# One block of full-row products, r turned in the outputs' banks, scores in quarters, and a growing lookahead in a recurrence followed by experts

## The chip, the cores and the metric

The kernel runs on one core of a Trainium2 chip. The metric is the device time of one execution in microseconds. A core has a matrix engine (PE, with its weight loads counted apart as PEld), a vector engine (DVE), a scalar engine (ACT), a general engine (POOL) and a queue engine (SP) that issues transfers. Each engine works through its own instructions in the order in which the program gives them, and semaphores make one engine wait for another.

## What is computed

Two blocks follow each other. The first is a recurrence over 768 tokens for 4 batches and 8 heads of 48 elements, with a state that decays by `w` and a bonus `u` for the token's own term:

```python
for t in range(S):
    kt, vt, rt = (k[:, :, t], v[:, :, t], r[:, :, t])
    cur = np.einsum('bhd,bhe->bhde', u[None] * kt, vt)
    y[:, :, t] = np.einsum('bhd,bhde->bhe', rt, state + cur)
    state = w[None, :, :, None] * state + np.einsum('bhd,bhe->bhde', kt, vt)
```

Its output, seen as 3072 rows of 384, goes to a mixture of 16 experts in 4 groups of 4. Each row picks the best group and in it the best expert, and gets `combined * relu(x @ w1) @ w2` of that expert alone, where `combined` is the product of the two softmax weights.

```python
g_idx = np.argmax(g_logits, axis=1)
...
e_idx = np.argmax(e_logits, axis=1)
...
h = np.maximum(xg[mask_e] @ w1[g, e], 0.0)
ye = h @ w2[g, e]
...
out[tok_idx] = combined[:, None] * ye
```

## The kernel before, in words

The order of instructions on each engine is the order in which the program writes them; no scheduler moves them. Waits on PSUM go by what was written or read there before.

*The recurrence.* The tokens are cut into 24 blocks of 128, four batches by six stretches of time. Block `n` belongs to batch `n % 4`, and two neighbouring blocks form a pair whose `r`, `k` and `v` are loaded together. One step `s` of the main loop (L708) finishes block `s` and prepares later ones. For each block these pieces are needed:

- `scaled` (POOL): k divided by the decay, into `kp`. `own` (POOL): r times k times u, in two products, into `dg`.
- `turn(n, "kT")` and `turn(n, "rT")` (L442): four 128x128 transposes on PE each, into the bank `TR`; `turn_out` copies k out with ACT and multiplies r by the decay `pw` with DVE.
- `sum_own` (L435, DVE): sums `dg` over a head's elements to `du`, the token's own term. `diagonal(n, e)` (L480, ACT): four products each that write identity times `du` into `am`, so that a block has eight.
- `scores` (L460, PE): eight products of k by r, 48 rows deep, two of them side by side in the upper and lower half of the rows, into `PA`. `mask` (L470, DVE): copies the later tokens' scores over `am`, which has the diagonal by then.
- `state` (L489, PE): the carried state times r, into `YB`. `values` (L501, PE): `am` times v, added to it. `update` (L510, PE): k times v, into the bank `MS`. `carry` (L521, DVE): decays and adds the state. `values_out` (L532, ACT): copies `YB` to `yT`.

*The routing.* `rows_out` (L547) transposes `yT` back into rows (`RW`) and ACT copies them to `xt`. `gate_parts` (L536) multiplies `yT` by the gates' weights into the first 128 columns of `MS`, ACT copies that to `lT`, and `gate_sum` (L563) adds its four parts into the logits, other columns of `MS`. Every four steps a chunk of 512 rows is routed by `route_1` to `route_4` on DVE, with `route_e` on ACT and `route_p` on PE. `route_5` scatters the rows into regions of `x_sorted` by POOL, one tile per step from a list `late`. `fill` writes zeros into the ends of the regions, on SP, in steps 1 to 4.

*The experts.* From step 16 the first two experts' weights are requested piece by piece. After the last routing the 16 experts run one after the other, `up` (L868) and `down` (L883), with rows gathered by SP and results scattered by POOL.

PSUM has eight banks: `PA` and `YB` two each, `TR`, `RW`, `MS` and `SB` one each. In `YB` the results take 256 of 512 columns of each bank (`y_ps`).

In the loop before, a steady step gives PE: results, update, turn k of block `s + 3`, rows of block `s - 1`, scores of block `s + 2`, gate parts, turn r of block `s + 3`, prefix sums if due, gate sum of block `s`, state of block `s + 1`. DVE gets: carry, the own term's sum for `s + 3`, routing, mask, turned r. ACT gets: copy of the results, turned k, rows, four diagonal products, `lT`, four diagonal products. Step 0 also prepares block 2, and in steps 0 and 1 the sum comes after the turn of r (`begun`, L756).

Of the kernel before, what the change touches and what calls it, by code (L numbers as in the profile page):

```python
# [13 lines left out]
OP = mybir.AluOpType  # L14
# [3 lines left out]
P = 128  # L18
# [9 lines left out]
def kernel(  # L28
# [13 lines left out]
    nc = tc.nc  # L42
# [180 lines left out]
    with ExitStack() as rec:  # L223
# [11 lines left out]
        MS = ps([P, 512], "MS")  # L235
        SB = ps([P, 512], "SB")
        y_ps = YB[:, :, 0 : 2 * P]

        spare_at = [0]

# [37 lines left out]
        def load_half(t, src, g, a, queue):  # L278
            c, b = g // 2, 2 * (g % 2) + a
            queue.dma_start(out=t[:, a], in_=src[b, :, P * c : P * (c + 1), :].rearrange("h t d -> t h d"))  # L280
# [16 lines left out]
        for a in range(2):  # L297
            load_half(raw[0, "k"], k, 0, a, both[a])
            load_half(raw[0, "r"], r, 0, a, both[1 - a])
        zeros = ring.tile([P, XW], FP32, name="zeros")  # L300
        warm = ring.tile([P, 1], FP32, name="warm")
        nothing = ring.tile([P, 1], FP32, name="nothing")
        nc.vector.memset(nothing, 0.0)
        nc.scalar.activation(warm, nothing, AF.Exp)
        nc.scalar.dma_start(
            out=ub.rearrange("p h d -> p (h d)"), in_=bass.AP(tensor=u.tensor, offset=u.offset, ap=[[0, P], [1, H * D]])
        )
        raw[0, "v"] = load(v, 0, "vt", 4)
        raw[1, "r"] = load(r, 1, "rt", 3)
        raw[1, "k"] = load(k, 1, "kt", 3)  # L310
# [63 lines left out]
        def fill(i):  # L374
            for lo in range(FILL[0], FILL[1], 64):
                nc.sync.dma_start(
                    out=xs_reg[4 * i : 4 * i + 4, lo : lo + 64, :].rearrange("e n w -> n e w"),
                    in_=spread(zeros[64 * (i % 2) : 64 * (i % 2 + 1)], 1, 4),
                )
# [60 lines left out]
        turned = {}  # L440

        def turn(n, name, bank=None, early=False):  # L442
            ps = turned[n, name] = TR if bank is None else bank
            src = (kp if name == "kT" else rp)[(n // 2) % NKP]
            for hc in range(HC):
                two = src[:, n % 2, 2 * hc : 2 * hc + 2, :].rearrange("p e x -> p (e x)")
                nc.tensor.transpose(ps[:, hc, :], two, ident)  # L447
            if not early:
                turn_out(n, name)

        def turn_out(n, name):
            ps = turned.pop((n, name))
            dst = pool.tile([P, HC, P], FP32, tag=name, bufs=5 if name == "rT" else 4, name=name)
            rkT[n, name] = dst
            if name == "kT":
                nc.scalar.copy(dst, ps)  # L456
            else:
                nc.vector.tensor_tensor(out=dst, in0=ps, in1=pw, op=OP.mult)  # L458

        def scores(n):  # L460
            kT, rT = rkT.pop((n, "kT")), rkT[n, "rT"]
            for hc in range(HC):
                for e in range(2):
                    rows = slice(DP * e, DP * e + D)
                    nc.tensor.matmul(  # L465
                        PA[:, e, P * hc : P * (hc + 1)], lhsT=kT[rows, hc, :], rhs=rT[rows, hc, :],
                        start=True, stop=True, skip_group_check=True,
                    )

        def mask(n):  # L470
            nc.vector.copy_predicated(  # L471
# [4 lines left out]
        def diagonal_here(n):  # L476
            du = dus[n].rearrange("p (hc e) -> p e hc", e=2)
            nc.vector.copy_predicated(am[n % NAM][:, 0], spread(id_ps, 1, HC).bitcast(I32), spread(du[:, 0], 2, P))

        def diagonal(n, e):  # L480
            du = dus[n].rearrange("p (hc e) -> p e hc", e=2)
            for hc in range(HC):
                nc.scalar.mul(am[n % NAM][:, e, hc, :], ident, du[:, e, hc : hc + 1])  # L483
# [48 lines left out]
        def values_out(n):  # L532
            yT = yTs[n] = pool.tile([P, 2, 2, P], FP32, tag="yT", bufs=3, name="yT")
            nc.scalar.copy(yT.rearrange("p e j t -> p e (j t)"), y_ps)  # L534

        def gate_parts(n):  # L536
            yT = yTs[n]
            for q in range(NQ):
                e, j = q // 2, q % 2
                nc.tensor.matmul(  # L540
                    MS[32 * q : 32 * (q + 1), 0:P], lhsT=gwp[:, 4 * j + e, :], rhs=yT[:, e, j, :],
                    start=True, stop=True, skip_group_check=True,
                )
            lT = mid[n] = pool.tile([P, P], FP32, tag="lT", bufs=3, name="lT")
            nc.scalar.copy(lT, MS[:, 0:P])

        def rows_out(n):  # L547
            yT = yTs[n]
# [136 lines left out]
        turn_out(0, "rT")  # L685
        scaled_here(0, 1)
        nc.scalar.copy(T2, RWT)
        turn(1, "rT", YB[:, 0].rearrange("p (h t) -> p h t", t=P))
        sum_own(0)
        diagonal_here(0)  # L690
        scores(0)
        turn(1, "kT")
        diagonal(0, 1)
        mask(0)
        own(0, 1)
        scaled(1, 0)
# [5 lines left out]
        own(1, 1)  # L702
        scaled(2)
        same = ring.tile([P, HC], FP32, name="same")
        LA = 3
        late = []
        left = []
        for s in range(NT):  # L708
            g = s // 2 + 2
            if s % 2 == 0 and g < NG:  # L710
                if g + 1 < NG:
                    raw[g + 1, "k"] = load(k, g + 1, "kt", 3)
                    raw[g + 1, "r"] = load(r, g + 1, "rt", 3)
                raw[g, "v"] = load(v, g, "vt", 4)
            for job in left[0 : 1 if s < 18 else 2]:
                job()
            del left[0 : 1 if s < 18 else 2]
            if s % 2 == 0 and g < NG:
                if g > 2:
                    scaled(g)  # L720
                own(g, None, 0)
            if s % 2 == 1 and g < NG:
                own(g, None, 1)
            for c, i in late[0 : 1 if s < 22 else 2]:
                route_5(c, (i,))
            del late[0 : 1 if s < 22 else 2]
            if s == 0:
                nc.gpsimd.memset(zeros, 0.0)
            if s == 1:
                late_consts()  # L730
            if s == 3:
                consts()
            if s == 5:
                last_consts()
            if s in (1, 2, 3, 4):
                fill(s - 1)
            far = s + LA < NT
            values(s)
            update(s)
            values_out(s)  # L740
            for c in range(NB - 1):
                if s == 4 * c + 5:
                    route_e(c)
            carry(s)
            if s == 0:
                sum_own(1)
                diagonal_here(1)
                diagonal(1, 1)
                scores(1)
                mask(1)  # L750
                turn(2, "kT")
                turn(2, "rT")
                sum_own(2)
                diagonal(2, 0)
                diagonal(2, 1)
            begun = s >= 2  # L756
            if far:
                turn(s + LA, "kT")
                if begun:
                    sum_own(s + LA)  # L760
            if s >= 1:
                rows_out(s - 1)
            for c in range(NB - 1):
                last = c == NB - 2
                if s == 4 * c + 4:
                    route_1(c)
                if s == 4 * c + 5:
                    route_2(c)
                if s == 4 * c + 6:
                    route_3(c)  # L770
                    if c == 2:
                        choose_two()
                if s == 4 * c + (6 if last else 7):
                    route_4(c)
                    late += [(c, i) for i in range(4)]
            if s == 15:
                for i in range(2):
                    e = at_sp(two_i[0:1, i : i + 1])
                    early[i] = weight_tiles()
                    left += [partial(early_piece, e, *early[i], j) for j in range(NPIECE)]  # L780
            if s + 2 < NT:
                scores(s + 2)
                mask(s + 2)
            if far and begun:
                diagonal(s + LA, 0)
            gate_parts(s)
            if far:
                turn(s + LA, "rT")
                if not begun:
                    sum_own(s + LA)  # L790
                    diagonal(s + LA, 0)
                diagonal(s + LA, 1)
            for c in range(NB - 1):
                if s == 4 * c + 5:
                    route_p(c)
                    if c == 2:
                        count(12)
            gate_sum(s)
            if s + 1 < NT:
                state(s + 1)  # L800
            if s == 0:
                nc.vector.tensor_tensor(out=same, in0=wcol, in1=wraw, op=OP.not_equal)
        c = NB - 1
        rows_out(NT - 1)
        for job in late:
            route_5(job[0], (job[1],))
# [397 lines left out]
```

## Time and profile before

| | |
|---|---|
| median of 3 runs | 445.26 us (443.38 to 446.50) |
| profiled execution | 445.16 us, span 443.4 us |
| granted PE clock | 0.966 of full speed on average |
| first results of the recurrence | 17.7 us |
| results of step 4, of step 20 | 48.7 us, 138.2 us |
| results of the last step | 151.8 us |
| first product of the experts | 171.8 us |
| last scatter of an output begins | 439.0 us |

Work of the four compute engines by stage (busy us, from the windows of the profile):

| stretch, us | PE | DVE | ACT | POOL | PE clock |
|---|---|---|---|---|---|
| 0 to 17.7 | 6.76 | 10.66 | 6.03 | 12.47 | half |
| 17.7 to 30 | 10.68 | 5.06 | 5.54 | 8.36 | half |
| 30 to 48.7 | 15.99 | 12.59 | 14.13 | 16.43 | full from 30.7 |
| 48.7 to 138.2 | 87.02 | 63.60 | 66.40 | 49.40 | full |
| 138.2 to 152 | 12.81 | 7.55 | 7.00 | 5.18 | full |
| 152 to 172 | 5.31 | 8.72 | 5.07 | 7.32 | half from 157 |
| 172 to 443 | 258.36 | 42.74 | 88.40 | 103.94 | full from 177.5 |

A line of the timeline gives the start in us from the span's start, the duration, the engine, the line of the kernel, the operation, the tile written and the tiles read, and the number of instructions merged; in brackets stands how long the engine had been idle before and whose end released it. The page cuts the span into 40 slices of 11.1 us, one digit each, in tenths of busy time.

### The profile page before, as it was taken

The page shows a single profiled execution, that of the slowest core. Times are in us where ns is not written, and L with a number is a line of the kernel's source. Part 1 is how long each engine was busy: PE and PEld are TensorE (multiplying, and loading weights), DVE is VectorE, ACT ScalarE, POOL GpSimd, SP SyncE. Part 2 cuts the span into 40 slices and gives each one's busy share as a digit, 9 for nine tenths or more (in the row PEclk, how much of TensorE's full clock was granted, in tenths as well). Part 3 has the DMA queues.
Part 4 walks back from the last instruction along what each step waited for, and adds up shares of the span by engine and source line. Part 5 has one row for each costly group of instructions (what it writes and reads, how often), then busy time and mean ns, then how long its engine had stood idle before and what let it go on. Part 6 is the DMA issues. An engine that isn't in the chain of part 4 may idle for free.

```text
span 443.4 us, 9627 instructions
## 1 busy us (share of the span) xinstructions
PE 396.9 (90%) x3506; PEld 371.5 (84%) x3506; DVE 150.9 (34%) x389; ACT 192.6 (43%) x461; POOL 203.1 (46%) x240
## 2 busy tenths in 40 slices
PE   3787999999999825999999999999999999999980
PEld 2666787878788614999999999999999999999970
DVE  6456676767776362020220220220220122022110
ACT  3358777777777303234243244243244334423410
POOL 6689536666643331023614524524523633452435
PEclk9999999999999955999999999999999999999995
DMA  9899997731996627397798898899998999999000
GB/s 151 118 192 215 189 184 149 148 84 38 197 270 174 213 85 168 76 250 167 226 267 180 233 273 178 237 256 208 245 275 178 251 266 214 252 259 258 21 23 25
DMA packets 122902, 81.97 MB, mean 185 GB/s; under 512 B 96420, under 2 KB 114020, under 8 KB 122848
## 3 DMA queue, kind: packets, MB, share of 16 engines
q1 hardware_dynamic: 114976, 70.98, 70.6%
q0 software_dynamic: 4960, 9.55, 7.7%
q10 hardware_dynamic: 2912, 0.77, 1.0%
q8 instruction: 29, 0.48, 0.5%
q14 instruction: 25, 0.20, 0.2%
HBM read 70.09 MB, written 11.68 MB: 184 GB/s over the span
## 4 chain that ended last, share of the span: by engine, by line
issue 45%; PE 26%; POOL 16%; DVE 4%; DMA 4%; ACT 3%; POOLq 1%; DVEq 0%; ACTq 0%
POOL out_dram L900 16%; PE TR L447 6%; PE YB L505 5%; PE PA L465 5%; DMA out_dram<-yt,idn 3%; PE YB L496 3%; PE MS L540 2%; ACT am L483 2%; PE MS L516 2%; PE RW L550 1%; PE MS L564 1%; POOL x_sorted L215 1%; DVE du L438 1%; DMA x_sorted<-xt,place_i 1%; DMA wraw<-in_w_dram 0%
## 5 line engine op out<-in xcount | busy, mean ns | idle before, releaser
L900 POOL DMA_INDIRECT out_dram<-yt,idn x107 | 103.9, 971 | 167.4 <-DVE yt L898 125.4
L876 PE MATMUL ph<-xe,w 128*128 128x200 f32 (+12 forms) x768 | 133.2, 334 | 8.1 <-DMA w<-in_moe_w_dram 8.1
L876 PEld LDWEIGHTS ph<-xe,w 128*128 128x128 f32 x768 | 130.3, 193 | 8.7 <-issue 8.1
L888 PE MATMUL po<-hT,w2p 128*128 128x200 f32 (+12 forms) x768 | 130.4, 330 | 0.0
L888 PEld LDWEIGHTS po<-hT,w2p 128*128 128x128 f32 x768 | 128.1, 190 | 0.0
L897 DVE STREAM_TRANSPOSE yt<-yT 128x672 f32<-128x672 f32 (+1 forms) x16 | 13.6, 847 | 211.1 <-ACT yT L891 211.1
L881 ACT ACTIVATE hT<-ph 128x416 f32<-128x416 f32 (+12 forms) x64 | 31.9, 498 | 101.9 <-PE ph L876 100.4
L483 ACT ACTIVATE am<-ident,du 128x128 f32<-128x128 f32 x184 | 58.6, 397 | 7.6 <-DVE du L438 7.6
L866 ACT COPY w2p<-w 128x1024 f32<-128x1024 f32 x48 | 47.0, 1046 | 11.9 <-POOL yT L823 11.9
L215 POOL DMA_INDIRECT x_sorted<-xt,place_i x24 | 24.0, 998 | 50.4 <-issue 43.9
L891 ACT COPY yT<-po 128x208 f32<-128x208 f32 (+12 forms) x48 | 15.5, 323 | 69.2 <-PE po L888 67.3
L471 DVE COPY_PREDICATED am<-later,PA 128x1024 f32<-128x1024 int32 x24 | 31.3, 1304 | 13.3 <-PE PA L465 7.6
L465 PE MATMUL PA<-rT,kT 48*128 48x128 f32 x384 | 30.6, 304 | 0.0
L505 PE MATMUL YB<-am,vt 128*48 128x128 f32 x384 | 26.8, 283 | 3.2 <-DVE am L471 3.2
L465 PEld LDWEIGHTS PA<-rT,kT 48*128 48x128 f32 x384 | 25.7, 204 | 4.3 <-issue 3.7
L505 PEld LDWEIGHTS YB<-am,vt 128*48 128x48 f32 x384 | 20.5, 125 | 7.4 <-DVE am L471 3.6
L534 ACT COPY yT<-YB 128x512 f32<-128x512 f32 x24 | 14.0, 584 | 28.0 <-PE YB L505 28.0
L431 POOL TENSOR_TENSOR kp<-kt,T 128x768 f32<-128x768 f32 x10 | 18.3, 1830 | 9.1 <-PE MS L516 4.6
L456 ACT COPY kT<-TR 128x512 f32<-128x512 f32 x24 | 14.0, 583 | 12.5 <-PE TR L447 12.0
L421 POOL TENSOR_TENSOR dg<-rp,kt 128x768 f32<-128x768 f32 x10 | 18.3, 1826 | 1.0 <-DMA rp<-in_r_dram 1.0
L423 POOL TENSOR_TENSOR dg<-dg,ub 128x768 f32<-128x768 f32 x10 | 18.3, 1827 | 0.4
L447 PE MATMUL TR<-ident,kp 128*128 128x128 f32 x96 | 17.6, 311 | 0.9 <-DVE rT L458 0.9
(140 smaller groups left out, 317.9 us busy)
## 6 DMA issues: line engine op xcount, KB each, us to landing
w<-in_moe_w_dram SPq DMA_DIRECT2D x128, 384.0 KB, 8.5
vt<-in_v_dram SPq DMA_DIRECT2D x24, 192.0 KB, 5.2
kt<-in_k_dram SPq DMA_DIRECT2D x23, 192.0 KB, 4.6
rp<-in_r_dram SPq DMA_DIRECT2D x23, 192.0 KB, 5.2
xg<-x_sorted SPq DMA_DIRECT2D x42, 85.8 KB, 4.7
out_dram<-yt,idn POOLq DMA_INDIRECT x107, 4.9
x_sorted<-zeros SPq DMA_DIRECT2D x4, 392.0 KB, 5.0
xg<-x_sorted SPq DMA_DIRECT2D x20, 73.5 KB, 5.1
```

The lines of the kernel that those rows point to most:

```text
L215: ins = nc.gpsimd.indirect_dma_start(out=xs_dram, out_offset=bass.IndirectOffsetOnAxis(ap=place_i[:, i : i + 1], axis=0), in_=xt[:, i].rea ...
L421: nc.gpsimd.tensor_mul(dg, rt, kt)
L447: nc.tensor.transpose(ps[:, hc, :], two, ident)
L465: nc.tensor.matmul(PA[:, e, P * hc : P * (hc + 1)], lhsT=kT[rows, hc, :], rhs=rT[rows, hc, :], start=True, stop=True, skip_group_check=True,)
L471: nc.vector.copy_predicated(am[n % NAM], later.unsqueeze(1).unsqueeze(1).to_broadcast([P, 2, HC, P]).bitcast(I32), PA.rearrange("p e (h t) ...
L483: nc.scalar.mul(am[n % NAM][:, e, hc, :], ident, du[:, e, hc : hc + 1])
L505: nc.tensor.matmul(y_at(e, hc), lhsT=vt[:, n % 2, 2 * hc + e, :], rhs=amn[:, e, hc, :], start=(n < 4 and hc < 2), stop=True, skip_group_ch ...
L866: nc.scalar.copy(o4[:, kk], v4[:, kk])
L876: nc.tensor.matmul(ph[:, i, 0:n], lhsT=w1[:, ko, P * (f + i) : P * (f + i + 1)], rhs=xe[:, ko].rearrange("p i b -> p (i b)")[:, 0:n], star ...
L881: nc.scalar.activation(hTs[s][:, f : f + 2, 0:n], ph[:, :, 0:n], AF.Relu)
L888: nc.tensor.matmul(po[:, 0:n], lhsT=w2p[:, d, fo, :], rhs=hT[:, fo, 0:n], start=(fo == 0), stop=(fo == FO - 1))
L900: ins = nc.gpsimd.indirect_dma_start(out=out_q, out_offset=bass.IndirectOffsetOnAxis(ap=idn[:, i : i + 1].bitcast(U32), axis=0), in_=yt[:, ...
```

## The change

- `turn` puts r into columns 256 to 511 of the outputs' two banks (`RT` in `YB`) instead of `TR`.
- `gate_parts` writes into the first 128 columns of `TR` (`lT_ps`) instead of `MS`.
- `scores` makes four products of each former two: the left and the right 64 columns of k, the right ones against the right 64 columns of r alone. Block 0 stays as it was.
- The order of a step: after `carry` come turn k, rows, turn r, gate sum (of the block before), prefix sums and gate parts; then routing; then scores, mask and state; and last the own term (`own_term`: the sum, then eight diagonal products).
- Steps 0 to 2 turn block `s + 2`, and step 2 also block 5; scores are one block ahead in steps 1 and 2, and step 3 makes up for the one that lacks. From step 3 on the lookahead is as it was.
- The load of `u` is issued between two halves of the first loads on ACT's queue; in the preparation the diagonal of block 0 goes ahead of the turns of block 1.
- The fills move to steps 4 to 7, the prefix sums one step later, and the scatters are taken one per step and four in the last.

```diff
+        RT = YB[:, :, 2 * P : 4 * P].rearrange("p b (h t) -> p b h t", t=P)
+        lT_ps = TR[:, 0, :]
...
+            if a == 0:
+                nc.scalar.dma_start(
+                    out=ub.rearrange("p h d -> p (h d)"),
+                    in_=bass.AP(tensor=u.tensor, offset=u.offset, ap=[[0, P], [1, H * D]]),
+                )
...
-            ps = turned[n, name] = TR if bank is None else bank
+            ps = (TR if name == "kT" else RT) if bank is None else bank
...
+                    for z in range(2):
+                        nc.tensor.matmul(
+                            PA[64 * z : 64 * (z + 1), e, P * hc + 64 * z : P * (hc + 1)],
+                            lhsT=kT[rows, hc, 64 * z : 64 * (z + 1)], rhs=rT[rows, hc, 64 * z : P],
+                            start=True, stop=True, skip_group_check=True,
+                        )
...
-                    MS[32 * q : 32 * (q + 1), 0:P], lhsT=gwp[:, 4 * j + e, :], rhs=yT[:, e, j, :],
+                    lT_ps[32 * q : 32 * (q + 1), :], lhsT=gwp[:, 4 * j + e, :], rhs=yT[:, e, j, :],
...
-        turn(1, "rT", YB[:, 0].rearrange("p (h t) -> p h t", t=P))
         sum_own(0)
         diagonal_here(0)
+        diagonal(0, 1)
+        turn(1, "rT", YB[:, 0].rearrange("p (h t) -> p h t", t=P))
         scores(0)
         turn(1, "kT")
-        diagonal(0, 1)
         mask(0)
...
-            for c, i in late[0 : 1 if s < 22 else 2]:
+            for c, i in late[0 : 1 if s < NT - 1 else 4]:
                 route_5(c, (i,))
...
-            if s in (1, 2, 3, 4):
-                fill(s - 1)
+            if s in (4, 5, 6, 7):
+                fill(s - 4)
+
+            def own_term(n):
+                sum_own(n)
+                diagonal(n, 0)
+                diagonal(n, 1)
...
             if s == 0:
                 sum_own(1)
                 diagonal_here(1)
                 diagonal(1, 1)
+            values(s)
+            update(s)
+            values_out(s)
+            carry(s)
+            if s == 0:
                 scores(1)
                 mask(1)
...
+            if s == 3:
+                scores(4)
+                mask(4)
+            far = s + (3 if s > 2 else 2)
+            if far < NT:
+                turn(far, "kT")
             if s >= 1:
                 rows_out(s - 1)
...
+            if far < NT:
+                turn(far, "rT")
+            if s >= 1:
+                gate_sum(s - 1)
+            for c in range(NB - 1):
+                if s == 4 * c + 6:
+                    route_p(c)
+                    if c == 2:
+                        count(12)
+            gate_parts(s)
...
+            ahead = s + (2 if s > 2 else 1)
+            if 0 < s and ahead < NT:
+                scores(ahead)
+                mask(ahead)
             if s + 1 < NT:
                 state(s + 1)
+            if far < NT:
+                own_term(far)
+            if s == 2:
+                turn(5, "kT")
+                turn(5, "rT")
+                own_term(5)
...
+        gate_sum(NT - 1)
         rows_out(NT - 1)
```

More of the change, by code (lines that the diff above doesn't have):

```diff
@@ L304 @@
         nc.scalar.activation(warm, nothing, AF.Exp)
-        nc.scalar.dma_start(
-            out=ub.rearrange("p h d -> p (h d)"), in_=bass.AP(tensor=u.tensor, offset=u.offset, ap=[[0, P], [1, H * D]])
-        )
         raw[0, "v"] = load(v, 0, "vt", 4)
@@ L442, in turn @@
         def turn(n, name, bank=None, early=False):
-            ps = turned[n, name] = TR if bank is None else bank
+            ps = (TR if name == "kT" else RT) if bank is None else bank
+            turned[n, name] = ps
             src = (kp if name == "kT" else rp)[(n // 2) % NKP]
@@ L446, in turn @@
                 two = src[:, n % 2, 2 * hc : 2 * hc + 2, :].rearrange("p e x -> p (e x)")
-                nc.tensor.transpose(ps[:, hc, :], two, ident)
+                dst = ps[:, hc, :] if len(ps.shape) == 3 else ps[:, hc // 2, hc % 2, :]
+                nc.tensor.transpose(dst, two, ident)
             if not early:
@@ L456, in turn_out @@
                 nc.scalar.copy(dst, ps)
-            else:
-                nc.vector.tensor_tensor(out=dst, in0=ps, in1=pw, op=OP.mult)
+            elif len(ps.shape) == 3:
+                nc.vector.tensor_tensor(out=dst, in0=ps, in1=pw, op=OP.mult)
+            else:
+                nc.vector.tensor_tensor(
+                    out=dst.rearrange("p (b h) t -> p b h t", b=2), in0=ps,
+                    in1=pw.rearrange("p (b h) t -> p b h t", b=2), op=OP.mult,
+                )
         def scores(n):
@@ L464, in scores @@
                     rows = slice(DP * e, DP * e + D)
[L465 to L468, printed above, removed]
+                    if n == 0:
+                        nc.tensor.matmul(
+                            PA[:, e, P * hc : P * (hc + 1)], lhsT=kT[rows, hc, :], rhs=rT[rows, hc, :],
+                            start=True, stop=True, skip_group_check=True,
+                        )
+                        continue
+                    for z in range(2):
+                        nc.tensor.matmul(
+                            PA[64 * z : 64 * (z + 1), e, P * hc + 64 * z : P * (hc + 1)],
+                            lhsT=kT[rows, hc, 64 * z : 64 * (z + 1)], rhs=rT[rows, hc, 64 * z : P],
+                            start=True, stop=True, skip_group_check=True,
+                        )
         def mask(n):
@@ L544, in gate_parts @@
             lT = mid[n] = pool.tile([P, P], FP32, tag="lT", bufs=3, name="lT")
-            nc.scalar.copy(lT, MS[:, 0:P])
+            nc.scalar.copy(lT, lT_ps)
         def rows_out(n):
@@ L704 @@
         same = ring.tile([P, HC], FP32, name="same")
-        LA = 3
         late = []
@@ L723 @@
                 own(g, None, 1)
-            for c, i in late[0 : 1 if s < 22 else 2]:
+            for c, i in late[0 : 1 if s < NT - 1 else 4]:
                 route_5(c, (i,))
-            del late[0 : 1 if s < 22 else 2]
+            del late[0 : 1 if s < NT - 1 else 4]
             if s == 0:
@@ L734 @@
                 last_consts()
-            if s in (1, 2, 3, 4):
-                fill(s - 1)
[L737 to L744, printed above, removed]
+            if s in (4, 5, 6, 7):
[4 more added lines that the diff above has]
+                diagonal(n, 1)
             if s == 0:
@@ L748 @@
                 diagonal(1, 1)
+            values(s)
[3 more added lines that the diff above has]
+            if s == 0:
                 scores(1)
                 mask(1)
[L751 to L760, printed above, removed]
+            if s == 3:
[4 more added lines that the diff above has]
+                turn(far, "kT")
             if s >= 1:
@@ L763 @@
             for c in range(NB - 1):
-                last = c == NB - 2
+                if s == 4 * c + 5:
+                    route_e(c)
+            if far < NT:
[8 more added lines that the diff above has]
+            gate_parts(s)
+            for c in range(NB - 1):
                 if s == 4 * c + 4:
@@ L772 @@
                         choose_two()
-                if s == 4 * c + (6 if last else 7):
+                if s == 4 * c + (6 if c == NB - 2 else 7):
                     route_4(c)
@@ L780 @@
                     left += [partial(early_piece, e, *early[i], j) for j in range(NPIECE)]
[L781 to L798, printed above, removed]
+            ahead = s + (2 if s > 2 else 1)
+            if 0 < s and ahead < NT:
+                scores(ahead)
+                mask(ahead)
             if s + 1 < NT:
                 state(s + 1)
+            if far < NT:
[4 more added lines that the diff above has]
+                own_term(5)
             if s == 0:
```

## The prediction

> **What bounds the kernel now.** I read the page first (busy times, slices, chain), then the chain in order of time, then the timeline of one steady step and of step 1. From the page:
>
> ```profile
> span 443.4 us, 9627 instructions
> ...
> PE 396.9 (90%) x3506; PEld 371.5 (84%) x3506; DVE 150.9 (34%) x389; ACT 192.6 (43%) x461; POOL 203.1 (46%) x240
> ...
> PE   3787999999999825999999999999999999999980
> ...
> PEclk9999999999999955999999999999999999999995
> ```
>
> Two stages with a hollow between them. The slices are 11.1 us each. Slices 0 to 13 are the recurrence (its products run from 17.7 to 153 us), and from 171.8 us the experts keep PE busy to the end. The change touches the recurrence and the zero fills alone; the experts begin after the last scatter, so what the recurrence gains or loses moves the end one for one. The profiled execution took 445.16 us (443.4 span, 1.7 around it), 0.1 from the median of 445.26, so the sum needs no correction.
>
> PE and DVE in a steady step, from the timeline (start, duration):
>
> ```profile
> 89.24 0.66 PE L447 MATMUL TR<-ident,kp 128*128 128x128 f32 x4
> ...
> 89.73 0.60 PE L550 MATMUL RW<-ident,yT 128*128 128x128 f32 x4
> ...
> 90.09 0.54 DVE L438 TENSOR_REDUCE du<-dg 128x8 f32<-128x384 f32 x1
> ...
> 90.26 1.16 PE L465 MATMUL PA<-rT,kT 48*128 48x128 f32 x16
> ...
> 91.35 0.43 PE L540 MATMUL MS<-yT,gwp 128*32 128x128 f32 x8
> 91.54 1.32 DVE L471 COPY_PREDICATED am<-later,PA 128x1024 f32<-128x1024 int32 x1 [0.51 <-PE PA L465]
> ...
> 91.71 0.66 PE L447 MATMUL TR<-ident,rp 128*128 128x128 f32 x4
> ...
> 92.27 0.40 PE L564 MATMUL MS<-sel,lT 128*128 128x20 f32 x2
> ...
> 92.60 0.66 PE L496 MATMUL YB<-rT,R 48*48 48x128 f32 x16
> ...
> 93.18 1.08 PE L505 MATMUL YB<-am,vt 128*48 128x128 f32 x16
> ```
>
> PE never waits: its starts follow each other, and a step is 93.18 - 87.87 = 5.31 us. With the routing's steps the mean from step 4 to step 20 (48.7 to 138.2) is 5.60. The sum `du` runs on DVE before the mask (90.09 against 91.54), so ACT has it long before it fills the diagonal.
>
> Step 1, where today's code still sums late, shows what ACT does with a late `du`:
>
> ```profile
> 31.52 0.54 DVE L438 TENSOR_REDUCE du<-dg 128x8 f32<-128x384 f32 x1
> ...
> 32.10 2.45 ACT L483 ACTIVATE am<-ident,du 128x128 f32<-128x128 f32 x8 [2.01 <-DVE du L438]
> ...
> 34.45 0.56 ACT L534 COPY yT<-YB 128x512 f32<-128x512 f32 x1
> ...
> 34.92 0.58 ACT L456 COPY kT<-TR 128x512 f32<-128x512 f32 x1
> ...
> 35.06 0.16 PEld L540 LDWEIGHTS MS<-yT,gwp 128*32 128x32 f32 x8 [0.83 <-ACT yT L534]
> ```
>
> ACT idles 2.0 us for `du`, then does eight diagonal products, and only then copies out the results; PE waits for that copy.
>
> **The change, part by part.**
>
> *PE's order.* By starts, a step today is: results 0.91, state sums 0.46, turn k 0.49, rows 0.53, scores 1.09, gate parts 0.36, turn r 0.56, gate sum 0.33, carried state 0.58. In one block, rows, turn r and gate sum follow each other without a change of shape. A turn's four products are 0.11 apart (0.60 = 3 x 0.11 + 0.27), so rows and turn r are 0.44 each. The gate sum no longer waits for `lT`, which is a step old. The step's PE work is then 0.91 + 0.46 + 0.49 + 0.44 + 0.44 + 0.33 + 0.36 + scores + state.
>
> *Scores in quarters.* Eight products become sixteen. The nearest row is the carried state, four tiles at once, 16 instructions in 0.58, rounds of four 0.11 apart. Each row half still streams eight times 128 columns: 8 x 0.11 + 0.04 = 0.91. Bounds: 0.91, or half as much again (1.36) if the 64-column pieces do not run beside the others. I take 0.91, the carried state's form being nearly the same. State then follows in the same shape, 0.53. Sum 4.87 us, a gain of 0.44 if PE stays the limit.
>
> *The own term moves behind the mask.* This decides. Today `sum_own(s + 3)` stands ahead of routing and mask on DVE. After the change `own_term` comes last in the step: on DVE the sum is queued behind `mask(s + 2)`, the mask waits for `scores(s + 2)`, and these now come after `gate_parts(s)`, which needs `yT(s)`. On ACT the eight diagonal products wait for the sum, and behind them is queued `values_out(s + 1)`, which makes `yT(s + 1)`. Turn r, now in the outputs' banks, waits for that copy too (today the gate parts wait for DVE's reads elsewhere in their own bank, so the wait goes by banks). The ring closes once a step. Its length, each link from a row where the second waited for the first:
> yT to PE 0.61 (34.45 to 35.06); turn r to gate sum 0.49 (as turn k); gate sum 0.33; gate parts 0.36; scores to mask 1.2 (90.26 to 91.54, less 0.09 for the lighter first load); mask to the next on DVE 1.15 (86.28 to 87.43); sum to the first diagonal 0.58 (31.52 to 32.10); eight diagonals to yT 2.35 (32.10 to 34.45). Together 7.07 us a step, against 4.87 of PE work, which it hides.
>
> It runs in steps 3 to 20, 18 rounds: 127.3 us.
>
> *Routing.* In the ring DVE has 1.0 us between r's product and the mask. Route 1 takes 1.2 (+0.2, five times), route 2 1.67 (+0.66, four), route 3 and the choice of two +0.4. The prefix sums stand ahead of the gate parts on PE: 0.5 each, five times, and the count 0.3. Together 6.8. Today's reads of the logits that hold up the gate parts (2.1 us by the waits) go, but PE waits anyway.
>
> *The first steps.* `ub` is loaded about a microsecond sooner (POOL waits 2.0 us for it, ended at 9.49), and the diagonal of token block 0 is filled before k of block 1 is copied. The mask of step 0 then waits for the scores (13.5) in place of ACT (16.3), so its results begin near 14.9, not 17.7. Step 0 turns one pair fewer: step 1's results start at about 22.5 (30.9 today, where PE waits 1.3 us for POOL's scaled keys and turns two pairs). Steps 1 and 2 already run the ring, at half clock in part (about 8.5 each), and step 2 holds two own terms (16 products, 4.7 us): results of step 2 near 31.1, of step 3 near 39.6, scores of step 5 near 46.1. Today these begin at 45.8. The start's gain is eaten by then.
>
> *The end.* Steps 21 to 23 have no own term: from scores of step 23 to the results of step 23, 0.91 + 0.53, then copy, gate parts, state (1.8 + 0.36 + 0.55), 4.2 us. The four scatters go to step 23; POOL has 5.6 us idle there. The fills move from steps 1-4 to 4-7, on SP behind the loads, land in 5 us and are needed at step 8: nothing.
>
> *Sum.* Results of step 23 start at 46.1 + 127.3 + 6.8 + 4.2 = 184.4; today 151.8. So +32.6, and 445.2 + 32.6 = 478.
>
> *PE's clock* is not in it. In the ring PE waits 7.07 - 4.87 = 2.2 us in one piece each step. The trace has the clock fall at 157 us, after
>
> ```profile
> 154.69 0.64 PE L550 MATMUL RW<-ident,yT 128*128 128x128 f32 x4
> 156.77 0.52 PE L176 MATMUL MS<-ohe,later 128*128 128x64 f32 x2 [1.45 <-DVE ohe L167]
> ```
>
> when PE was busy 1.51 of 3.40 us; it kept full speed with 2.30 of 3.40 busy (41.0 to 44.4). The worst 3.4 us in the ring have about 1.2 to 1.5 busy, so it can fall in places. At half clock the ring's PE links grow by about 1.8 us (scores 2.0 for 1.1 at 27.09, turns 1.02 for 0.56). Bounds: 0 and 18 x 1.8 = 32; I take 0 for the likeliest, since a slowed PE fills its own wait and gets the clock back, as at 30.7, and keep up to 20 for the range.
>
> The Trainium skill (TensorE: Matmul & The Clock Gate, "Why this matters for your kernels") puts the fall at idle gaps of about 3 us. Here it fell after gaps of 1.5 us at most, so the row speaks for a fall that the rule would exclude; by the rule the sum stays 478.
>
> **The rivals.**
>
> *Faster: PE stays the limit.* If the own term were ready in time, the step would be 4.87 plus 0.1 of routing: 18 x (5.60 - 4.97) = 11 us less, and about 4 from the first steps: 430. It decides if scores to the end of yT's wait (1.2 + 1.15 + 0.58 + 2.35 + 0.61 = 5.89) falls below PE's own way from scores to turn r (0.91 + 0.53 + 0.91 + 0.46 + 0.49 + 0.44 = 3.74). For it: PE never waits today. Against it: 2.15 us are missing, and step 1 shows the order kept. Chance 0.06.
>
> *Turned r does not wait for the copy* (waits by columns, not banks). Then gate parts wait for k's copy alone, whose bank they now share: 0.47 + 0.62 = 1.09 in place of 1.43; 18 x 0.34 = 6 less: 472. Chance 0.12.
>
> *Quarters that run one after the other:* 18 x 0.45 = 8 more: 486. Chance 0.12.
>
> *The clock falls in part of the rounds:* 10 to 20 more, 488 to 498. Chance 0.25.
>
> **How the numbers follow.** The ring as summed has the other 0.45: 478, give or take 5 for the first steps. The range runs from 466 (finer waits and a better start) to 498; under it lies the faster case, above it a clock that falls everywhere. Slower by over 1% (what a measurement here can tell from no change) 0.93, within 1% 0.02, faster 0.05.
>
> **What would show it.** Steps of 7 to 7.5 us between 46 and 180 us; ACT idle some 2 us a step before `am<-ident,du`, ended by `du`; the results' copy starting right after eight diagonal products; PE idle about 2 us before the turn of r, ended by ACT's yT; PE busy near 70% in slices 4 to 16; scores at 0.9 us. Wrong if ACT's wait for `du` is missing, if steps are near 5 us, or if the scores take over 1.3 us.

## The result, and the profile after

The changed kernel takes 476.84 us (474.01 to 478.98, 4 runs) against 445.87 for the kernel before, measured beside it: a ratio of 1.0702, 95% interval 1.0631 to 1.0773. The profiled execution took 478.98 us, span 477.2, and is the longest of the four.

The page of the changed kernel, its totals, the slices of PE and of its clock, and the chain by engine and line:

```profile
span 477.2 us, 10295 instructions
...
PE 404.6 (85%) x3874; PEld 382.5 (80%) x3874; DVE 150.1 (31%) x389; ACT 192.2 (40%) x461; POOL 203.5 (43%) x240
...
PE   3778777688777887179999999999999999999990
...
PEclk9987899987798779669999999999999999999995
...
issue 41%; PE 19%; POOL 16%; ACT 12%; DVE 7%; DMA 4%; POOLq 1%; ACTq 0%; DVEq 0%
```

The chain of the kernel before:

```profile
issue 45%; PE 26%; POOL 16%; DVE 4%; DMA 4%; ACT 3%; POOLq 1%; DVEq 0%; ACTq 0%
```

ACT and DVE do the same work as before, and the chain now goes through them: 12% and 7%, against 3% and 4%. PE's slices in the recurrence fell from 9 to between 6 and 8, and its clock, full there before, has gaps. The results of step 23 start at 186.1 us, 34.3 later than before; from there to the experts' first product it is 20.1 us (20.1 before), and from that to the end 271.0 (271.6). So all of the loss is in the recurrence.

One step of it, from the timeline (start, duration; two rounds of scores are 7.00 us apart):

```profile
72.00 0.99 PE L483 MATMUL PA<-rT,kT 48*64 48x128 f32 x30
...
73.17 1.32 DVE L490 COPY_PREDICATED am<-later,PA 128x1024 f32<-128x1024 int32 x1 [0.40 <-PE PA L483]
...
74.38 0.54 DVE L442 TENSOR_REDUCE du<-dg 128x8 f32<-128x384 f32 x1
...
74.95 2.45 ACT L502 ACTIVATE am<-ident,du 128x128 f32<-128x128 f32 x8 [2.49 <-DVE du L442]
...
77.31 0.56 ACT L553 COPY yT<-YB 128x512 f32<-128x512 f32 x1
...
77.92 0.66 PE L453 MATMUL YB<-ident,rp 128*128 128x128 f32 x4 [1.99 <-ACT yT L553]
...
78.64 0.43 PE L559 MATMUL TR<-yT,gwp 128*32 128x128 f32 x8
...
79.00 0.99 PE L483 MATMUL PA<-rT,kT 48*64 48x128 f32 x30
```

This is the ring, link by link: scores, mask, sum, eight diagonals, the results' copy, the turn of r (PE idle 2.0 us before it), gate parts, scores. The waits between 48 and 176 us name the same two places (total, times, longest):

```profile
ACT am L502 <- DVE du L442: 47.4, 16, 3.4
...
PEld YB L453 <- ACT yT L553: 32.9, 17, 2.9
```

### The profile page after: what moved, and what is told of

Its sections match the earlier page's. It is cut to its first block, busy times and chain, and to the rows that moved or that the text cites. A ratio compares the mean times of both kernels' runs of the same rounds, so it can differ in the third digit from the quotient of the medians.

```text
span 477.2 us, 10295 instructions
## 1 busy us (share of the span) xinstructions
PE 404.6 (85%) x3874; PEld 382.5 (80%) x3874; DVE 150.1 (31%) x389; ACT 192.2 (40%) x461; POOL 203.5 (43%) x240
## 4 chain that ended last, share of the span: by engine, by line
issue 41%; PE 19%; POOL 16%; ACT 12%; DVE 7%; DMA 4%; POOLq 1%; ACTq 0%; DVEq 0%
POOL out_dram L922 15%; ACT am L502 10%; PE PA L483 6%; DVE am L490 4%; PE YB L453 3%; DMA out_dram<-yt,idn 3%; PE YB L524 2%; ACT yT L553 2%; PE TR L559 2%; DVE du L442 1%; PE TR L453 1%; PE MS L583 1%; POOL x_sorted L215 1%; PE RW L569 1%; PE YB L515 1%
## 5 line engine op out<-in xcount | busy, mean ns | idle before, releaser
L502 ACT ACTIVATE am<-ident,du 128x128 f32<-128x128 f32 x184 | 56.4, 389 | 59.9 <-DVE du L442 59.9
L453 PE MATMUL YB<-ident,rp 128*128 128x128 f32 x92 | 16.8, 311 | 31.4 <-ACT yT L553 31.4
L453 PEld LDWEIGHTS YB<-ident,rp 128*128 128x128 f32 x92 | 11.0, 153 | 35.9 <-ACT yT L553 35.9
L524 PE MATMUL YB<-am,vt 128*48 128x128 f32 x384 | 32.1, 321 | 3.8 <-DVE am L490 2.3
L524 PEld LDWEIGHTS YB<-am,vt 128*48 128x48 f32 x384 | 24.9, 145 | 9.9 <-issue 4.9
L483 PE MATMUL PA<-rT,kT 48*64 48x128 f32 (+1 forms) x736 | 31.8, 294 | 0.0
L466 DVE TENSOR_TENSOR rT<-YB,pw 128x512 f32<-128x512 f32 x22 | 15.2, 690 | 50.8 <-PE YB L453 45.5
L483 PEld LDWEIGHTS PA<-rT,kT 48*64 48x64 f32 x736 | 25.0, 157 | 5.2 <-issue 5.1
L515 PE MATMUL YB<-rT,R 48*48 48x128 f32 x320 | 21.4, 333 | 0.0
```

The costliest lines, as they stand in the source:

```text
L453: nc.tensor.transpose(dst, two, ident)
L483: nc.tensor.matmul(PA[64 * z : 64 * (z + 1), e, P * hc + 64 * z : P * (hc + 1)], lhsT=kT[rows, hc, 64 * z : 64 * (z + 1)], rhs=rT[rows, hc ...
L515: nc.tensor.matmul(y_at(e, hc), lhsT=R[n % 4][rows, hc, :], rhs=rT[rows, hc, :], start=(hc < 2), stop=False, skip_group_check=True,)
L524: nc.tensor.matmul(y_at(e, hc), lhsT=vt[:, n % 2, 2 * hc + e, :], rhs=amn[:, e, hc, :], start=(n < 4 and hc < 2), stop=True, skip_group_ch ...
```

## The experiments

Times below are medians. The runs were on several chips, and on one of them the kernel before took 460.9 us instead of 445, so a time is compared with the others of its chip, or by the length of a step in the trace.

**1. The sum ahead of routing and mask** (`e1_sum_early`). On the changed kernel:

```diff
             if far < NT:
                 turn(far, "kT")
+                if s > 2:
+                    sum_own(far)
...
             def own_term(n):
-                sum_own(n)
+                if n not in dus:
+                    sum_own(n)
```

> The changed kernel with one move: from step 3 on the own term's sum goes on DVE right behind the turn of k, ahead of routing and mask; the eight diagonal products stay at the step's end. Theory (the ring through mask, sum, diagonal and copy): the ring opens, ACT no longer waits for du (47.4 us in the waits of the changed kernel), steps fall from 7.8 us to 4.7 to 5.0, time 425 to 435 us, below the kernel before. Rival (the turn of r in the outputs' banks makes PE wait for the results' copy, wherever the sum stands): PE still waits some 2 us a step for yT, time above 465 us.

425.8 us, kernel before 444.8: 0.9589 (0.9549 to 0.9630). One instruction per step, moved, is worth some 51 us (51.6 where both ran on one chip, experiments 5 and 7), and the rest of the change is a gain. PE in the steady step:

```profile
66.63 1.08 PE L524 MATMUL YB<-am,vt 128*48 128x128 f32 x16
67.54 0.53 PE L535 MATMUL MS<-vt,kp 128*48 128x48 f32 x16
68.00 0.66 PE L453 MATMUL TR<-ident,kp 128*128 128x128 f32 x4
68.49 0.60 PE L569 MATMUL RW<-ident,yT 128*128 128x128 f32 x4
68.93 0.60 PE L453 MATMUL YB<-ident,rp 128*128 128x128 f32 x4
69.36 0.30 PE L583 MATMUL MS<-sel,lT 128*128 128x20 f32 x2
69.59 0.43 PE L559 MATMUL TR<-yT,gwp 128*32 128x128 f32 x8
69.95 0.99 PE L483 MATMUL PA<-rT,kT 48*64 48x128 f32 x30
70.67 0.31 PE L515 MATMUL YB<-rT,R 48*48 48x128 f32 x2
...
71.41 0.86 PE L524 MATMUL YB<-am,vt 128*48 128x128 f32 x11
```

No bracket: PE waits for nobody, and a step is 71.41 - 66.63 = 4.78 us, 5.31 before. ACT's wait for `du` is gone from its list of waits, and so is PE's for the results' copy.

**2. The scores ahead of the turn of r** (`e2_scores_first`). The block `scores(ahead); mask(ahead)` moves from behind the routing to a place between rows and turn r; nothing else.

> The changed kernel with the scores and the mask moved ahead of the turn of r; the own term stays behind the mask. Theory: a ring needs both, a sum behind the mask and scores behind what waits for yT. With the scores ahead of that wait the ring closes once in two steps, about 9.8 us, 4.9 a step, near PE's own work: 425 to 440 us. Rival (a sum behind the mask is late by itself, since ACT's copy is queued behind eight products): little gain, above 465 us.

449.1 us, 1.0097 of the kernel before (1.0059 to 1.0135). Six of the seven per cent lost come back, so the rival is wrong: the sum stands behind the mask as late as ever. But 449 is above what was expected, and the trace names a ring that I had not counted:

```profile
67.16 1.10 PE L483 MATMUL PA<-rT,kT 48*64 48x128 f32 x32
...
68.40 1.31 DVE L490 COPY_PREDICATED am<-later,PA 128x1024 f32<-128x1024 int32 x1 [1.40 <-PE PA L483]
...
69.60 0.68 DVE L466 TENSOR_TENSOR rT<-YB,pw 128x512 f32<-128x512 f32 x1
...
70.33 0.66 PE L515 MATMUL YB<-rT,R 48*48 48x128 f32 x16 [1.00 <-DVE rT L466]
...
73.31 1.10 PE L483 MATMUL PA<-rT,kT 48*64 48x128 f32 x32
```

r's product now stands behind the mask on DVE, it reads the outputs' banks, and the carried state, which writes them, waits for it. Link by link: scores to mask 1.24, mask to r's product 1.20, product to carried state 0.73, and 2.98 of PE's own order from there to the next scores: 73.31 - 67.16 = 6.15 us a step.

**3. The kernel before with the late sum** (`e3_before_sum_late`): `begun = s >= 2` becomes `begun = False`.

> The kernel before with the own term late in all steps (sum and eight diagonal products behind the mask and the turn of r). Theory: in that order the scores stand ahead of the gate parts, so the ring takes two steps for about 10.8 us, 5.4 a step against 5.3 of PE work: 445 to 455 us. Rival (the late sum alone costs what was measured): 470 to 485 us.

447.9 against 444.8 us, 1.0078 (1.0043 to 1.0113). ACT waits 22.3 us for `du` between 48 and 130 us, so the sum is late there too, but alone it costs about 0.8%. That it has two steps to come round where the scores precede the gate parts fits its steps, 5.70 us on average from step 4 to step 18 against 5.64 before; the links were not read one by one.

**4. PE kept busy in its wait** (`e4_busy`). On the changed kernel, ahead of the turn of r; the added products go into banks that the scores write afterwards:

```diff
+            if 2 < s and far < NT:
+                for i in range(10):
+                    nc.tensor.transpose(PA[:, 0, 0:P], ident, ident)
```

> The changed kernel with ten added transposes of the identity (1.1 us of PE at full clock) into the scores' banks ahead of the turn of r in steps 3 to 20, where PE waits some 2 us; nothing else. They add work that the output does not need. Theory: the ring's length does not go through them, and PE's clock falls less often, so the 18 steps lose what the half clock put on the ring's products, some 6 us: 468 to 474 us, mean clock over 0.94. Rival (the falls cost nothing, or the added products delay the ring): 476 us or more.

474.2 us, all four runs within 0.2, mean clock 0.953; the changed kernel's eight runs lie between 474.0 and 480.7 with 0.914 to 0.934. From the results of step 4 to those of step 22 the trace has 134.7 us, 138.7 without the added products. Plain steps are 7.0 us in both. So by the medians the falls of the clock cost some 3 to 5 us, a little less than was expected, and 6.5 us in the slowest run. Some falls are left in this trace too. That they also make the spread between runs fits, but was not tried by itself.

**5. Half of the diagonal out of the ring** (`e9_half_diagonal`, `e9_again`). On the changed kernel, with `owed` a list made ahead of the loop:

```diff
                 sum_own(n)
                 diagonal(n, 0)
-                diagonal(n, 1)
+                if s > 2:
+                    owed.append(n)
+                else:
+                    diagonal(n, 1)
...
             if far < NT:
                 turn(far, "kT")
+            for n in owed:
+                diagonal(n, 1)
+            owed.clear()
```

> The changed kernel; from step 3 on four of the eight diagonal products come in the next step, behind the copies of the results and of the turned k; the sum stays behind the mask. Theory: the ring loses four of its products, 4 x 0.29 = 1.2 us in each of 18 rounds, 21 us: 450 to 460 us. Rival (the end of the recurrence, the scatters or the start make the slowdown): 470 us or more.

458.9 us, but on the chip where the kernel before takes 460.9, so the time can't be set against the expectation. Plain steps in its trace are 5.90 us, 1.10 less than 7.00. So it ran again beside the changed kernel:

> The changed kernel once more, unaltered, beside the three that follow on one chip, since the last four ran on a chip on which the kernel before took 461 us. Theory and rival alike: 1.06 to 1.08 of the kernel before.

> The changed kernel with four of the eight diagonal products moved out of the ring, as first run, on this chip. Theory: 18 rounds 1.1 us shorter, as its first trace had them, so 17 to 24 us below the changed kernel beside it. Rival: less than 10 us below.

Changed kernel 479.3 us, 1.0736 (1.0682 to 1.0789); with half of the diagonal moved 455.9, 1.0254 (1.0217 to 1.0291): 23.5 us less for 18 x 4 products taken out of the ring, the products being executed all the same. The shorter ring by itself gives 18 x 1.10 = 19.8 of that. The rest goes with a clock that was granted more often (0.943 to 0.961 against 0.914 to 0.934), which this run doesn't separate.

**6. What the other parts are worth once the ring is open.** Whole scores (`e5_whole_scores`), r turned where it was (`e10_r_in_TR`: `RT = TR`, `lT_ps = MS[:, 0:P]`), both on experiment 1, and the quarters alone on the kernel before (`e7_before_quarters`):

> The kernel with the sum ahead of the mask (425.8 us), with the scores in whole products for all blocks, as in the kernel before. With the sum early PE sets the pace, so the scores' time counts: 1.09 us from scores to the next kind of work in the kernel before, 0.73 here, 23 times 0.36 to 0.45: 434 to 437 us. Rival (another engine sets the pace at 4.78 us a step): 426 us.

> The kernel with the sum ahead of the mask (425.8 us), with r turned in the bank of the turned k and the gate parts back in their old bank. PE then waits for ACT's copy of k before the turn of r, some 0.4 us a step in 21 steps: 431 to 436 us. Rival (the place of r matters only in the ring): 426 us.

> The kernel before with the scores in quarters from block 1 on, nothing else. PE sets the pace there: 23 times 0.27 to 0.36 us less, 436 to 439 us. Rival (the quarters bring their gain only next to the carried state, whose shape they share): 444 us or more.

On this chip: 438.6 (0.9529 of its 460.9; 0.9472 to 0.9585), 447.8 (0.9717; 0.9682 to 0.9753) and 459.5 us (0.9959; 0.9928 to 0.9990). By plain steps whole scores cost 5.00 against 4.78, so quarters are worth 0.22 a step, less than the 0.36 expected. The times don't show this gain (0.9529 with whole scores, 0.9589 and 0.9602 with quarters on other chips, the intervals overlapping); only the steps do. With r in the old bank a step is 5.24: PE waits for the copy of k, and 60.04 - 59.20 = 0.84 lie between rows and r's turn, 0.44 in experiment 1:

```profile
59.20 0.60 PE L569 MATMUL RW<-ident,yT 128*128 128x128 f32 x4
60.04 0.65 PE L453 MATMUL TR<-ident,rp 128*128 128x128 f32 x4 [0.24 <-ACT kT L462]
```

That was expected. In the order of before the quarters bring next to nothing, steps staying at 5.32: from scores to gate parts it is 1.03 us (84.76 to 85.79) for 1.09, and what is left PE gives back by waiting for `lT`. So the run came out near its rival, that quarters pay where the carried state follows in the same shape; the shape was not tried apart from the order.

**7. The best version, again and one step further** (`e1_again`; `e8_sum_early_1` also takes step 1, `if s == 1 or s > 2`).

> The changed kernel with the sum ahead of routing and mask, as first run, on this chip. Theory (PE sets the pace in both): 0.95 to 0.965 of the kernel before, whatever the chip. Rival (its gain was one chip's): above 0.98.

> The kernel with the sum ahead of the mask, and the sum ahead also in step 1, where POOL has the product of block 3 by 20.4 us and DVE is free from 21 us. Theory: step 1 of this kernel still runs the ring (7.0 us), so up to 2 us less than the kernel beside it. Rival (the next steps wait for POOL's keys of block 4, 24.5 to 26.3 us, anyway): the same within 1 us.

427.8 us, 0.9602 (0.9566 to 0.9639), and 425.4, 0.9556 (0.9527 to 0.9585), kernel before 445.2. So the gain of experiment 1 holds on a second chip. Step 1 is not shown to matter: the intervals overlap, and the results of step 4 start at 42.22 us in its trace, 42.23 and 43.28 in the two of experiment 1.

## Why the prediction was right

*The ring* was the mechanism, and every link is within 0.11 us of its estimate: scores to mask 1.17 (1.2 predicted), mask to sum 1.21 (1.15), sum to diagonal 0.57 (0.58), diagonal to copy 2.36 (2.35), copy to turn 0.61 (0.61), turn 0.50 (0.49), gate sum 0.22 (0.33), gate parts 0.36 (0.36); 7.00 in place of 7.07. Experiments 1 and 5 show that it is the cause and not a companion: opened it gives back 51 us, shortened by 1.1 us in 18 rounds it gives back 23.5, of which 19.8 are the ring's own.

*Turned r waits for the copy by banks*, as taken; the rival that it would not wait falls with the 32.9 us for which the weight loads of r's turn waited for `yT`.

*Scores in quarters:* scores and state were put at 0.91 + 0.53 = 1.44 us and take 71.41 - 69.95 = 1.46 in experiment 1. The rival of quarters one after another falls.

*PE's own step:* 4.87 predicted, 4.78 measured once the ring is open. The faster rival had the right price for its case: 430 us predicted, 425.8 and 427.8 measured.

*Two sizes were off and cancelled,* so that 478 lies so near to 476.8 is in part luck. The scores of step 5 start at 41.5 us, not 46.1: the step "at half clock in part (about 8.5 each)" failed, for PE was at full speed from 12.6 to 26.3 us, where the kernel before was at half until 30.7: step 0 took 4.6 us and not 7.6, step 1 6.9 and not 8.6. Step 2, with half clock from 26.3 to 29.7, took the 8.5 predicted. (The `PEclk` line reads 9 in the first slices of both kernels, and the mean clocks count this time as full, because the trace has no record of the clock before its first change; the speed is read from the products, here the first results of the kernel before and of the changed one.)

```profile
17.70 1.95 PE L505 MATMUL YB<-am,vt 128*48 128x128 f32 x16 [3.19 <-DVE am L471]
...
14.50 1.08 PE L524 MATMUL YB<-am,vt 128*48 128x128 f32 x16 [0.86 <-DVE am L490]
```

The 18 rounds took 140.0 us, not 127.3 + 6.8 = 134.1: the step that put the clock's falls at 0 failed. PE ran at half clock for about 43 of these 140 us. Routing is not the reason: with few falls (experiment 4) four steps of a chunk take 6.99 + 7.26 + 8.18 + 7.00 = 29.4 us, 1.4 above four plain ones, as summed. The end took 4.6 us for 4.2. Together 32.6 predicted and 34.3 traced. PE's busy share between 41.4 and 176 us is 79% (105.7 of 134.6 us), not near 70%: products at half clock keep it busy longer.

*The clock rival* was half right: the falls came, but cost 3 to 8 us and not 10 to 20 (2.6 and 5.1 by the two medians against experiment 4; 4.0 and 7.7 by the results of step 4 to step 22 in the two traces of the changed kernel), for they slow only the few products behind PE's wait, about 0.8 us in the step in which one came (102.25 to 110.05), and a PE that works longer is soon at full clock again.

## What to carry to other kernels

Before moving an instruction to a later place, write down what stands ahead of it and behind it on its own engine, and follow the waits until they close; the length of the ring, not the busy time of any engine, is then the step. Here each move alone was cheap (the late sum 0.8%, scores behind the gate parts no bound once the sum is early) and together they closed a ring of 7.0 us over 4.8 us of work. A PSUM bank shared by two uses adds links that no data dependence shows: r in the outputs' banks, with the gate parts in the place it left, was worth 0.46 us a step where nothing waited behind it, and closed a ring of 6.15 us when the mask stood ahead of it.

## What the runs showed of the hardware that was not expected

*PE's clock falls without a long gap.* Stretches of 3.4 us of the changed kernel, from the windows of the profile (length; busy us of PE, PEld, DVE, ACT, POOL; granted clock; transfers):

```profile
91.10:94.51 3.41, 1.64 (x22) 1.37 (x26) 0.84 (x2) 2.58 (x8) 0.00 (x0) 1.00 0.03 5
94.51:97.93 3.42, 3.42 (x56) 3.05 (x58) 2.25 (x6) 0.27 (x1) 0.00 (x0) 0.50 0.31 60
97.93:101.34 3.41, 2.21 (x37) 1.92 (x34) 0.96 (x3) 3.13 (x10) 0.00 (x0) 1.00 0.38 71
...
104.75:108.17 3.42, 1.43 (x26) 1.14 (x22) 1.14 (x3) 2.96 (x10) 3.19 (x4) 1.00 0.15 59
108.17:111.58 3.41, 3.40 (x46) 2.98 (x50) 1.73 (x6) 1.20 (x4) 3.33 (x2) 0.50 0.16 59
111.58:114.99 3.41, 3.41 (x50) 3.02 (x46) 1.74 (x2) 1.11 (x4) 3.13 (x3) 0.50 0.19 64
```

Here a stretch with PE busy for less than half ends in a half clock for the next one or two; one with 2.21 of 3.41 us busy does not. There is no sharp bound: in the same trace the stretch from 22.83 us with 1.99 us busy was followed by half clock, the one from 67.21 us with 1.73 was not. PE's longest idle piece in the stretches shown is about 2 us, and 2.7 in its waits for `yT` between 48 and 176 us. The Trainium skill (TensorE: Matmul & The Clock Gate, "Why this matters for your kernels") asks that no idle gap exceed about 3 us; in these runs that was not enough.

*One chip was slower late in the recurrence.* Where the kernel before took 460.9 us, the results of step 21 came 8.9 us after those of step 20 with whole scores, 9.0 with r in the old bank and with quarters alone, and 4.4 to 5.1 us on the others in the kernel before and in experiment 1. PE stood idle 2.0 us at 130 us in the first of these without a wait that the profile shows, while the experts' first weights were being loaded. The cause was not tried.
